# Talking-heads attention and a mixture of experts on one core: first transfers over two queues, six score buffers, due times a step sooner, loads by their use

## The chip, the cores and the metric

The kernel runs on 1 core of one Trainium2 chip. The metric is the device time of one execution in microseconds, the median of several runs; lower is better.

## The reference, cut to what matters

```python
# q, k, v: (4, 12, 448, 64); w_pre, w_post: (12, 12)
scores = (q @ k.transpose(0, 1, 3, 2)) / sqrt(64)
scores = einsum('bhij,hg->bgij', scores, w_pre)      # pre-mix: heads mixed ahead of the softmax
scores = scores - max(scores, -1)
attn = exp(scores); attn = attn / (sum(attn, -1) + 1e-9)
attn = einsum('bhij,hg->bgij', attn, w_post)         # post-mix: heads mixed behind it
x = (attn @ v)                                       # as 1792 tokens of 768
# then: x goes to one of 8 experts, the arg max of cosine similarities over tau
out[mask] = gate[mask] * (relu(x[mask] @ w1[e]) @ w2[e])
```

All of it is float32. The change touches the attention alone.

## The kernel before

**Tiles and pairs.** The 448 query rows of each of the 4 batches are cut into 4 tiles of 120, 120, 120 and 90 rows: 16 tiles (`NTL`). The 12 heads are taken as 6 pairs a tile: 96 pairs. `emit_qk` (L228) computes the scores of one pair, four matmuls into two PSUM banks: one `ps_q` tile (one buffer), or, in the opening for odd pairs, two `ps_p` tiles (two buffers of one bank). Its `evict` copies them into a score buffer `s` (`s_p`, 4 buffers, L139), on ACT, or for odd pairs of the opening on DVE. Its `place` (L247) sends that buffer with two DMAs on SP's queue, one for each head, into the tile's group buffer (`group(t)`, one of three), in which partitions hold (query row within ten, head), so that the heads can be mixed by a matmul. A group buffer is written again for a later tile once the tile before it in that buffer is read.

**Steps.** Each tile is then read in steps of 20 query rows (6, 6, 6 and 5 steps, 92 in all, `steps`; `first[t]` is tile t's first: 0, 6, 12, 18, 23, 29, ...). For step s: `emit_pre` (L261) mixes the heads into `ps_p`, `emit_max` takes row maxima on DVE (L274), `emit_exp` exponentials on ACT with row sums (L283), `emit_r` the reciprocals on DVE and with them the post weights `wr` on GpSimd (L294), `emit_post` (L299) mixes again and transposes on TensorE, DVE copies the result to `a` (L322), `emit_av` multiplies by v a tile later.

**Opening.** Lines 729 to 759 are in the order in which each engine gets its instructions: q of tile 0 and the six k of batch 0 on SP; 8 filler matmuls (`NWARM`); then `N0` = 9 pairs, each evicted and placed while the next is computed, with q of tile 1 loaded on SP after the placing of pair 2 (`i == 3`); q of tile 2, the ninth pair's placing, four loads of v; 20 filler matmuls (`NWAIT`); then pre-mix, maximum and exponentials of step 0, the same of step 1, and the reciprocals of step 0.

**The loop over steps** (L768): all engines run in order, and the order is written out by hand. In step s: up to one pair ahead of, and one behind, the rest; `emit_pre(s + 2)`; the copy of step s - 1; that pair's eviction and placing; `emit_post(s)`; `emit_max` and `emit_exp` of s + 2; work of the tile before; at its end the loads listed in `bg` for this step. How many pairs are due by step s is the largest of `N0 + s + 1`, of `due(s)` (L760), which wants the last pair of tile t in step first[t] - 4, and of 96 + 3 (s - `OPEN`) // 2, which has all 96 done in step `OPEN` = 79, when the buffers of q, k and s are given up for expert weights. Loads are listed by L697 to L705: q of tile t (from 3 on) in step 6 t - N0 - 6, k of pair a in step 6 t + a - N0 - 6, the four parts of v in steps first[t + 1] - 6 to first[t + 1] - 3.

**Queues.** SP issues every load and every score transfer in the order of the program; a DMA whose target or source isn't free yet holds up those behind it.

Of the kernel before, what the change touches and what calls it, by code (L numbers as in the profile page):

```python
# [7 lines left out]
F32 = mybir.dt.float32  # L8
# [18 lines left out]
NTL = 4 * B  # L27
# [4 lines left out]
LEAD = 2  # L32
N0 = 9
NWAIT = 20
XW = 128 + E
# [9 lines left out]
def talking_heads_moe(  # L45
# [79 lines left out]
    with tc.manual_schedule():  # L125
# [12 lines left out]
        q_p = bx.enter_context(tc.tile_pool(name="q", bufs=3, side="right"))  # L138
        s_p = bx.enter_context(tc.tile_pool(name="s", bufs=4, side="right"))  # L139
        ve_p = bx.enter_context(tc.tile_pool(name="ve", bufs=1, side="right"))  # L140
# [23 lines left out]
        def embed():  # L164
# [41 lines left out]
            V.tensor_scalar(out=ioE_v, in0=ioE_v, scalar1=1.0, scalar2=None, op0=ALU.add)  # L206

        q_sb, k_sb, v_sb = {}, {}, {}

# [18 lines left out]
        def emit_qk(i, eng, pre=False):  # L228
# [10 lines left out]
            def evict():  # L239
                sb = s_p.tile([128, 2, S], F32, tag="s", name="s")  # L240
                for o, i in [(sb, pq[:, :, :S])] if pq is not None else [(sb[:, r], p[r][:, :S]) for r in range(2)]:
                    if eng is A:
                        A.activation(out=o, in_=i, func=ACTF.Copy)  # L243
                    else:
                        V.tensor_copy(out=o, in_=i)

                def place():  # L247
                    for r in range(2):
                        h = 4 + 2 * a + r
                        Y.dma_start(out=group(t)[h:h + 109:12, :n // 10].rearrange("p c s -> p (c s)"), in_=sb[:n, r])  # L250
                return place
# [8 lines left out]

        def emit_pre(s):  # L261
            t, m, nx = steps[s]
            p = [ps_p.tile([128, 512], F32, tag="p", name="p_p") for _ in range(2)]
            g = group(t)
# [432 lines left out]
        for t in range(NTL):  # L697
            b, ti = divmod(t, 4)
            if t:
                bg_at(max(6 * t - N0 - 6, 0), lambda t=t: load_q(t)) if t > 2 else None  # L700
            if ti == 0 and b:
                for a in range(NPAIR):
                    bg_at(max(6 * t + a - N0 - 6, 0), lambda b=b, a=a: load_k(b, a))
                for jt in range(4):
                    bg_at(first[t + 1] - 6 + jt, lambda b=b, jt=jt: load_v(b, jt))  # L705
# [34 lines left out]
        for g in gb[1:]:  # L740
            G_.memset(g[:4], 0.0)
        pend = []
        for i in range(N0):
            pend.append(emit_qk(i, V if i % 2 else A, i % 2 == 1))
            if i:
                pend.pop(0)()()
            if i == 3:
                load_q(1)
        load_q(2)
        pend.pop()()()  # L750
        for jt in range(4):
# [3 lines left out]
        for s in range(LEAD):  # L755
            emit_pre(s)
            emit_max(s)
            emit_exp(s)
        run(emit_r(0))
        def due(s):  # L760
            n = [min(NPAIR * t + NPAIR, NPAIR * t + s + 10 - first[t]) for t in range(NTL) if s > first[t] - 10]
            return n + [NTL * NPAIR + 3 * (s - OPEN) // 2]

        qk_n = N0
        evict = None
        ea = None
        gv = None
        for s in range(ns):  # L768
            cr = emit_r(s + 1) if s + 1 < ns else iter(())
            evs = []  # L770
            want = min(NTL * NPAIR, max(N0 + s + 1, *due(s)))
            assert want - qk_n < 3
            if qk_n < want:
                evs.append(emit_qk(qk_n, A))
                qk_n += 1
# [5 lines left out]
            if evs:  # L781
                evs.pop()()()
            evict = emit_post(s)
# [9 lines left out]
            if evs:  # L793
                evs.pop()()()
            for f in pes.pop(s, ()):
# [357 lines left out]
```

## Time and profile before

| | us |
|---|---|
| median of 3 runs | 762.78 |
| lowest and highest of them | 761.76, 764.29 |
| the profiled execution | 760.22 |
| its span, first to last instruction | 758.4 |

The profile is of one execution. Its page gives busy times, the span in slices, DMA queues and the costliest groups of instructions; the trace can be asked for waits, for a timeline and for windows. PE is TensorE's matmuls, PEld its weight loads, DVE VectorE, ACT ScalarE, POOL GpSimd; a "q" behind an engine's name is its queue, which issues DMAs. Matmuls of float32 are recorded twice, as two passes. TensorE's two clock levels are 1.2 and 2.4 GHz; "granted" is the share of the higher one.

### The profile page before, as it was taken

What the parts mean: (1) busy time and instruction counts of PE and PEld (TensorE: products, weight loads), DVE (VectorE), ACT (ScalarE), POOL (GpSimd) and SP (SyncE); (2) the same over time, 40 slices, a digit from 0 to 9 for tenths busy, and PEclk for the clock granted to TensorE, in tenths of its full rate; (3) what the DMA queues carried; (4) which work ended last, traced back from release to release, by engine and by line L of the source; (5) the groups of instructions that cost most, each with busy time, mean ns of one, the idle gap of its engine ahead of it and who ended that gap; (6) DMA issues with size and microseconds to landing.
All of it is one profiled execution on the core that took longest, in us unless ns stands there. A gap on an engine that the chain in (4) does not pass through costs nothing. (4 is left out here: it accounts for less than half of the span.)

```text
span 758.4 us, 26020 instructions
## 1 busy us (share of the span) xinstructions
PE 698.4 (92%) x11146; PEld 569.0 (75%) x11146; DVE 462.5 (61%) x1083; ACT 392.9 (52%) x767; POOL 118.1 (16%) x179
## 2 busy tenths in 40 slices
PE   5889999899999999969888978999999999999984
PEld 2557677566766767745566757999999999999973
DVE  3287666565765656634797464676866556565661
ACT  2366667566766766745444433453434436353550
POOL 9011100001000110100201024202020221201010
PEclk9899999999999999998989999999999999999997
DMA  6754555646556465662513172776758576756760
GB/s 201 235 159 150 168 160 170 201 134 173 177 176 179 131 202 171 189 191 85 190 56 85 56 254 74 224 242 206 233 184 260 185 253 187 239 193 194 228 208 15
DMA packets 55414, 133.09 MB, mean 175 GB/s; under 512 B 6519, under 2 KB 31239, under 8 KB 55296
## 3 DMA queue, kind: packets, MB, share of 16 engines
q1 hardware_dynamic: 51744, 118.94, 51.0%
q0 software_dynamic: 3520, 12.44, 5.0%
q8 instruction: 89, 1.46, 0.8%
q14 instruction: 29, 0.24, 0.1%
q10 hardware_dynamic: 32, 0.01, 0.0%
HBM read 81.64 MB, written 12.20 MB: 124 GB/s over the span
## 5 line engine op out<-in xcount | busy, mean ns | idle before, releaser
L274 DVE TENSOR_REDUCE mn<-p_p 128x1 f32<-128x448 f32 (+1 forms) x184 | 106.6, 618 | 120.1 <-PE p_p L266 119.7
L550 ACT ACTIVATE wh<-raw_w 128x768 fp32r<-128x768 f32 (+2 forms) x132 | 115.1, 904 | 52.5 <-DMA raw_w<-w 46.5
L283 ACT ACTIVATE e<-p_p,mn 128x448 f32<-128x448 f32 (+1 forms) x184 | 114.9, 629 | 49.2 <-DVE mn L274 44.9
L243 ACT ACTIVATE s<-p_q 128x896 f32<-128x896 f32 x92 | 84.4, 917 | 106.6 <-PE p_q L236 86.3
L551 DVE TENSOR_TENSOR wl<-raw_w,wh 128x768 fp32r<-128x768 f32 (+2 forms) x132 | 130.9, 1027 | 12.1 <-ACT wh L550 11.5
L309 PEld LDWEIGHTS p_m<-wr,e 64*64 64x64 f32 x4320 | 97.3, 137 | 51.6 <-issue 47.4
L236 PE MATMUL p_q<-k,q 64*64 64x448 f32 x768 | 97.8, 577 | 17.5 <-DMA q<-qT 14.7
L309 PE MATMUL p_m<-wr,e 64*64 64x60 f32 x4320 | 99.8, 224 | 8.3 <-DVE a L322 6.5
L266 PE MATMUL p_p<-g,wpre_sb 64*64 64x448 f32 (+1 forms) x720 | 93.0, 555 | 7.4 <-DMA v<-vP 3.5
L322 DVE COPY a<-p_m 128x420 f32<-128x420 f32 (+1 forms) x184 | 98.1, 574 | 0.8 <-PE p_m L314 0.7
L944 PE MATMUL p_h<-xh,wh 128*128 128x256 f32 x336 | 96.6, 288 | 0.0
L335 PE MATMUL p_av<-a,v 128*64 128x120 f32 (+1 forms) x1536 | 96.1, 271 | 0.0
L944 PE MATMUL p_h<-xh,wl 128*128 128x256 f32 x336 | 94.8, 282 | 0.0
L944 PE MATMUL p_h<-xl,wh 128*128 128x256 f32 x336 | 94.5, 281 | 0.0
L294 POOL TENSOR_TENSOR wr<-wpost_sb,r 128x120 f32<-128x120 f32 (+1 forms) x92 | 35.3, 383 | 348.2 <-DVE r L293 314.8
L335 PEld LDWEIGHTS p_av<-a,v 128*64 128x64 f32 x1536 | 76.7, 140 | 10.9 <-issue 5.4
L962 PE MATMUL p_o<-wh,hh 128*128 128x384 f32 x224 | 75.6, 338 | 0.0
L962 PE MATMUL p_o<-wl,hh 128*128 128x384 f32 x224 | 74.9, 334 | 0.0
L962 PE MATMUL p_o<-wh,hl 128*128 128x384 f32 x224 | 74.9, 334 | 0.0
L946 ACT ACTIVATE hh<-p_h 128x512 fp32r<-128x512 f32 x28 | 16.8, 598 | 100.8 <-PE p_h L944 79.9
L266 PEld LDWEIGHTS p_p<-g,wpre_sb 64*64 64x64 f32 (+1 forms) x720 | 30.0, 135 | 48.6 <-issue 28.4
L944 PEld LDWEIGHTS p_h<-xl,wh 128*128 128x128 f32 x336 | 63.6, 189 | 0.0
(205 smaller groups left out, 989.5 us busy)
## 6 DMA issues: line engine op xcount, KB each, us to landing
g<-s SPq DMA_DIRECT2D x144, 210.0 KB
raw_w<-w SPq DMA_DIRECT2D x54, 512.0 KB
raw_w<-w SPq DMA_DIRECT2D x72, 384.0 KB
g<-s SPq DMA_DIRECT2D x48, 157.5 KB
q<-qT SPq DMA_DIRECT2D x16, 384.0 KB
v<-vP SPq DMA_DIRECT2D x16, 384.0 KB
k<-kT SPq DMA_DIRECT2D x24, 224.0 KB
x_tok<-xs SPq DMA_DIRECT2D x12, 360.0 KB
```

The source lines that it names most:

```text
L236: T.matmul(p[r][64 * w:64 * w + 64, :S], q_sb[t][64 * r:64 * r + 64, a, w, :], k_sb[t // 4, a][64 * r:64 * r + 64], start=True, stop=True)
L243: A.activation(out=o, in_=i, func=ACTF.Copy)
L266: T.matmul(p[w][64 * x:64 * x + 64, :S], wpre_sb[64 * w:64 * w + 64 - 4 * w], g[64 * w:64 * w + 64 - 4 * w, m + x if nx == 2 else m], star ...
L274: V.tensor_reduce(out=mn[q, c:c + 1], in_=p[u][q, :S], op=ALU.max, axis=AX.X, negate=True)
L283: A.activation(out=e[q, c], in_=p[u][q, :S], func=ACTF.Exp, bias=mn[q, c:c + 1], accum_out=sums[q, c:c + 1])
L309: T.matmul(pm[x][q[c], u * 210 + jt * 60:u * 210 + jt * 60 + 60], e[q[x], u, jt * 128 + 64 * c:jt * 128 + 64 * c + 64], wr[q[x], u], start ...
L322: V.tensor_copy(out=a[:, :, m + x] if n == 2 else a[:, :, m, x], in_=src if n == 2 else src[:, :, 0])
L335: T.matmul(p[64 * r:64 * r + 64], v_sb[t // 4][:, jt, (2 * a + r) * D:(2 * a + r + 1) * D], a_sb[t % 2][:, c:c + n], start=jt == 0, stop=j ...
L550: A.activation(out=h[:, c], in_=r[:, c], func=ACTF.Copy)
L551: lo = lambda: eng.tensor_tensor(out=l[:, c], in0=r[:, c], in1=h[:, c].bitcast(F32), op=ALU.subtract)
L944: T.matmul(p[:, f], lt[:, c], rt_[:, k], start=(k == 0 and i == 0), stop=(k == KD - 1 and i == 2))
L962: T.matmul(p[:, :384], lt[:, k, c], rt_[:, m], start=(k == 0 and i == 0), stop=(k == KF - 1 and i == 2))
```

## The change

- `N0` is 10 and `NWAIT` 8.
- The score buffers `s` are 6.
- `place` takes a second queue for the second of its two DMAs: ACT's for the six pairs of tile 0, SP's as before for all others.
- q of tile 1 is loaded ahead of the opening's loop.
- In the opening both pre-mixes come first, the second into a `ps_q` tile, then maximum and exponentials of step 0, the reciprocals of step 0, maximum and exponentials of step 1.
- In the due times, 11 stands for 10: the last pair of a tile is due in step first[t] - 5. Step 0 has no pair ahead of its pre-mix.
- Score transfers go on a list (`held`) and are issued in order once the step has come (`free`) in which the last pre-mix of the tile before in the same group buffer is issued.
- `qk_at` holds the step in which each pair is computed, and q and k are loaded six steps before.

```diff
--- before.py
+++ after.py
@@ -30,8 +30,8 @@
 MAXO = 12
 NPAIR = H // 2
 LEAD = 2
-N0 = 9
-NWAIT = 20
+N0 = 10
+NWAIT = 8
 XW = 128 + E
 OPEN = 79
 NW = 4
@@ -136,7 +136,7 @@
         sm = ax.enter_context(tc.tile_pool(name="sm", bufs=4))
         k_p = bx.enter_context(tc.tile_pool(name="k", bufs=9, side="right"))
         q_p = bx.enter_context(tc.tile_pool(name="q", bufs=3, side="right"))
-        s_p = bx.enter_context(tc.tile_pool(name="s", bufs=4, side="right"))
+        s_p = bx.enter_context(tc.tile_pool(name="s", bufs=6, side="right"))
         ve_p = bx.enter_context(tc.tile_pool(name="ve", bufs=1, side="right"))
 
         gb = [p.tile([128, c, S], F32, name=f"g{i}") for i, (p, c) in enumerate(((ve_p, 12), (big, 12), (big, 9)))]
@@ -205,6 +205,19 @@
             yield
             V.tensor_scalar(out=ioE_v, in0=ioE_v, scalar1=1.0, scalar2=None, op0=ALU.add)
 
+        def due(s):
+            n = [min(NPAIR * t + NPAIR, NPAIR * t + s + 11 - first[t]) for t in range(NTL) if s > first[t] - 11]
+            return min(NTL * NPAIR, max(N0 + s + 1, NTL * NPAIR + 3 * (s - OPEN) // 2, *n))
+
+        def free(i):
+            t = i // NPAIR
+            back = 4 if t % 4 == 3 else 2 if t % 4 == 2 else 3
+            return first[t - back + 1] - 1 - LEAD if t >= back else 0
+
+        qk_at = [0] * N0
+        for s in range(OPEN + 1):
+            qk_at += [s] * (due(s) - len(qk_at))
+
         q_sb, k_sb, v_sb = {}, {}, {}
 
         def load_q(t):
@@ -244,10 +257,10 @@
                     else:
                         V.tensor_copy(out=o, in_=i)
 
-                def place():
+                def place(second=Y):
                     for r in range(2):
                         h = 4 + 2 * a + r
-                        Y.dma_start(out=group(t)[h:h + 109:12, :n // 10].rearrange("p c s -> p (c s)"), in_=sb[:n, r])
+                        (second if r else Y).dma_start(out=group(t)[h:h + 109:12, :n // 10].rearrange("p c s -> p (c s)"), in_=sb[:n, r])
                 return place
             return evict
 
@@ -258,9 +271,13 @@
             return [(slice(0, 128), u, u) for u in range(2)] if steps[s][2] == 2 else [
                 (slice(64 * w, 64 * w + 64), w, 0) for w in range(2)]
 
-        def emit_pre(s):
+        def emit_pre(s, pair=False):
             t, m, nx = steps[s]
-            p = [ps_p.tile([128, 512], F32, tag="p", name="p_p") for _ in range(2)]
+            if pair:
+                pq = ps_q.tile([128, 2, 512], F32, tag="q", name="p_q")
+                p = [pq[:, r] for r in range(2)]
+            else:
+                p = [ps_p.tile([128, 512], F32, tag="p", name="p_p") for _ in range(2)]
             g = group(t)
             for x, w in [(x, w) for w in range(2) for x in range(2)] if nx == 2 else [(0, 0), (1, 1)]:
                 T.matmul(p[w][64 * x:64 * x + 64, :S], wpre_sb[64 * w:64 * w + 64 - 4 * w],
@@ -697,10 +714,10 @@
         for t in range(NTL):
             b, ti = divmod(t, 4)
             if t:
-                bg_at(max(6 * t - N0 - 6, 0), lambda t=t: load_q(t)) if t > 2 else None
+                bg_at(max(qk_at[6 * t] - 6, 0), lambda t=t: load_q(t)) if t > 2 else None
             if ti == 0 and b:
                 for a in range(NPAIR):
-                    bg_at(max(6 * t + a - N0 - 6, 0), lambda b=b, a=a: load_k(b, a))
+                    bg_at(max(qk_at[6 * t + a] - 6, 0), lambda b=b, a=a: load_k(b, a))
                 for jt in range(4):
                     bg_at(first[t + 1] - 6 + jt, lambda b=b, jt=jt: load_v(b, jt))
         acts, dves, pes, avs = {}, {}, {}, {}
@@ -739,38 +756,37 @@
         next(ge)
         for g in gb[1:]:
             G_.memset(g[:4], 0.0)
+        load_q(1)
         pend = []
         for i in range(N0):
             pend.append(emit_qk(i, V if i % 2 else A, i % 2 == 1))
             if i:
-                pend.pop(0)()()
-            if i == 3:
-                load_q(1)
+                pend.pop(0)()(A if i <= NPAIR else Y)
+        pend.pop()()()
         load_q(2)
-        pend.pop()()()
         for jt in range(4):
             load_v(0, jt)
         for _ in range(NWAIT):
             T.matmul(p_w[:, :128], ones_sb, ones_sb, start=True, stop=True)
         for s in range(LEAD):
-            emit_pre(s)
+            emit_pre(s, s == 1)
+        for s in range(LEAD):
             emit_max(s)
             emit_exp(s)
-        run(emit_r(0))
-        def due(s):
-            n = [min(NPAIR * t + NPAIR, NPAIR * t + s + 10 - first[t]) for t in range(NTL) if s > first[t] - 10]
-            return n + [NTL * NPAIR + 3 * (s - OPEN) // 2]
-
+            if s == 0:
+                run(emit_r(0))
         qk_n = N0
+        held = []
+        placed = N0
         evict = None
         ea = None
         gv = None
         for s in range(ns):
             cr = emit_r(s + 1) if s + 1 < ns else iter(())
             evs = []
-            want = min(NTL * NPAIR, max(N0 + s + 1, *due(s)))
+            want = due(s)
             assert want - qk_n < 3
-            if qk_n < want:
+            if qk_n < want and s:
                 evs.append(emit_qk(qk_n, A))
                 qk_n += 1
             if s + LEAD < ns:
@@ -779,7 +795,10 @@
                 evict()
             next(cr, None)
             if evs:
-                evs.pop()()()
+                held.append(evs.pop()())
+            while held and free(placed) <= s:
+                held.pop(0)()
+                placed += 1
             evict = emit_post(s)
             next(cr, None)
             if qk_n < want:
@@ -791,7 +810,10 @@
                 emit_max(s + LEAD)
                 emit_exp(s + LEAD)
             if evs:
-                evs.pop()()()
+                held.append(evs.pop()())
+                while held and free(placed) <= s:
+                    held.pop(0)()
+                    placed += 1
             for f in pes.pop(s, ()):
                 f()
             for f in dves.pop(s, ()):
```

## Rows read from the trace of the kernel before

**Rows 1.** The page: busy us of each engine, share of the span, instructions
```profile
PE 698.4 (92%) x11146; PEld 569.0 (75%) x11146; DVE 462.5 (61%) x1083; ACT 392.9 (52%) x767; POOL 118.1 (16%) x179
```
**Rows 2.** Windows: stretch, length, busy us (instructions) of each engine, granted clock, DMA share, GB/s
```profile
60.00:136.00 76.00, 75.51 (x1932) 53.74 (x1926) 50.91 (x134) 52.39 (x120) 7.39 (x20) 1.00 0.57 168
...
380.00:400.00 20.00, 17.59 (x370) 13.40 (x370) 17.86 (x62) 9.75 (x28) 1.55 (x4) 0.83 0.17 49
```
**Rows 3.** TensorE's waits, 0 to 420 us: waiter, releaser, us in total, times, longest
```profile
PE p_q L236 <- DMA q<-qT: 14.7, 2, 9.0
...
PE p_p L266 <- DMA v<-vP: 3.5, 2, 2.0
```
**Rows 4.** DMA issues: what, queue, operation, count, KB each
```profile
g<-s SPq DMA_DIRECT2D x144, 210.0 KB
...
q<-qT SPq DMA_DIRECT2D x16, 384.0 KB
...
k<-kT SPq DMA_DIRECT2D x24, 224.0 KB
```
**Rows 5.** Timeline of the opening: start, us, engine, instruction, [idle time before <-releaser]
```profile
4.86 1.95 PE L236 MATMUL p_q<-k,q 64*64 64x448 f32 x16
...
12.56 1.57 SPq L212 DMA_DIRECT2D q<-qT  x1
12.89 0.92 ACT L243 ACTIVATE s<-p_q 128x896 f32<-128x896 f32 x1 [3.83 <-DMA g<-s]
14.24 11.84 SPq L250 DMA_DIRECT2D g<-s  x10
16.52 1.16 DVE L245 COPY s<-p_q 128x448 f32<-128x448 f32 x2 [6.51 <-DMA g<-s]
...
19.99 4.76 PE L236 MATMUL p_q<-k,q 64*64 64x448 f32 x24 [8.96 <-DMA q<-qT]
...
24.68 5.26 PE L754 MATMUL p_w<-ones_sb 128*128 128x128 f32 x40
...
29.87 0.98 PE L266 MATMUL p_p<-g,wpre_sb 64*64 64x448 f32 x8
```
**Rows 6.** Windows of the opening, columns as in rows 2
```profile
0.00:10.00 10.00, 8.55 (x58) 5.25 (x60) 4.57 (x9) 3.12 (x3) 8.86 (x14) 1.00 0.63 207
...
3.00:7.00 4.00, 3.78 (x25) 2.19 (x24) 2.09 (x2) 0.88 (x1) 4.00 (x2) 1.00 1.01 358
8.00:18.00 10.00, 2.94 (x28) 0.91 (x22) 2.31 (x4) 1.83 (x2) 10.00 (x8) 0.88 0.62 180
...
22.00:24.00 2.00, 2.00 (x16) 0.44 (x8) 0.72 (x2) 0.78 (x1) 0.00 (x0) 0.50 0.68 240
...
15.60:25.80 10.20, 5.81 (x29) 2.45 (x30) 2.31 (x4) 1.83 (x2) 3.04 (x1) 0.50 0.69 205
```
**Rows 7.** Timeline of ACT's queue, DMA issues
```profile
404.83 2.07 ACTq L450 DMA_DIRECT2D g_tok<-gt__7091  x3
```
**Rows 8.** Timeline of the first steps
```profile
34.94 0.39 POOL L294 TENSOR_TENSOR wr<-wpost_sb,r 128x120 f32<-128x120 f32 x1 [16.30 <-DVE r L293]
```
**Rows 9.** Timeline at late pre-mixes; last, a group of lines, 60 to 330 us
```profile
139.33 0.98 PE L266 MATMUL p_p<-g,wpre_sb 64*64 64x448 f32 x8 [1.95 <-DMA v<-vP]
...
233.05 0.98 PE L266 MATMUL p_p<-g,wpre_sb 64*64 64x448 f32 x8 [0.40 <-DMA g<-s]
...
323.79 0.98 PE L266 MATMUL p_p<-g,wpre_sb 64*64 64x448 f32 x8 [1.53 <-DMA v<-vP]
...
L274 DVE TENSOR_REDUCE mn<-p_p 128x1 f32<-128x448 f32 (+1 forms) x135 | 78.3, 619 | 92.7 <-PE p_p L266 92.6
```
**Rows 10.** Timeline and windows around pair 90
```profile
337.32 0.50 SPq L212 DMA_DIRECT2D q<-qT  x1
342.03 1.77 PE L236 MATMUL p_q<-k,q 64*64 64x448 f32 x8 [5.71 <-DMA q<-qT]
...
342.00:346.70 4.70, 4.67 (x80) 2.81 (x80) 1.38 (x4) 2.02 (x5) 0.00 (x0) 0.50 0.06 19
```

## The prediction

> **What bounds the kernel now.** I read the page's busy shares first: TensorE is busy for 92% of the span [rows 1], so a change that moves no arithmetic can only win back stretches in which TensorE stands still or runs at the lower clock. The windows by stretch tell where those are: from 60 to 136 us TensorE is busy 75.51 of 76 us, in the opening and late in the attention it is not [rows 2, 6]. The list of TensorE's waits up to 420 us, longest first, names them: 14.7 us for the loads of q in two places, and 3.5 us in front of a pre-mix (L266), for DMAs that the list names v [rows 3]. The timeline puts a place on each. In the opening TensorE waits 8.96 us for q of tile 1 at 19.99, then runs 20 filler matmuls (40 records, 5.26 us) and reaches the first pre-mix at 29.87 [rows 5]. Three first pre-mixes of a tile start late, at 139.33, 233.05 and 323.79, with 1.95, 0.40 and 1.53 us of idle time [rows 9]. At 342.03 the score matmul of pair 90 has waited 5.71 us for q of tile 15 [rows 10]. Elsewhere TensorE is the bound itself, so time that is won ahead of such a stretch is kept; nothing after it starts by a clock of its own.
>
> **A. The opening.** What must land before the first pre-mix can run is q and k of the first batch, 384 + 6 x 224 KB, q of tile 1 where it is queued ahead, and the 12 transfers of the six score pairs of tile 0, 210 KB each [rows 4].
> The kernel before spends this way: SP issues the transfers of three pairs, then q of tile 1 at 12.56, then ten more up to 26.08 [rows 5]. ACT's fifth eviction and DVE's third wait 3.83 and 6.51 us for a score buffer whose transfer has not landed [rows 5]: four buffers throttle the issue. The pairs 6 to 8 wait for q, and behind them stand the fillers. So before, no single thing is the bound; it is a relay of three.
> After the change q of tile 1 stands at about 4 us in SP's queue, straight behind k; the six pairs of tile 0 have a buffer each, so no eviction of tile 0 waits for a landing; one transfer of each such pair goes through ACT's queue.
> How soon can all of it have landed? From 0 to 10 us 207 GB/s were moved, 2.07 MB [rows 6], of which q and k are 1.77 MB, so some 0.3 MB are others' (GpSimd's loads and the first scores). Left at 10 us are about 12 x 0.215 + 0.39 - 0.25 = 2.7 MB, and some 0.15 MB of GpSimd's small loads. At 205 GB/s, as from 15.6 to 25.8 us [rows 6], that is 14 us, landing at 24; at 240, the best stretch [rows 6], 12 us, landing at 22. I take 23.
> Is TensorE there by then? Even pairs share one PSUM buffer, so each takes its matmuls (0.98, as eight matmuls of that width take [rows 9]) and its eviction (0.92 on ACT [rows 5]) in turn, 2.0 us with the hand-over; for the first six pairs ACT issues two transfers between two of its evictions. An issue on ACT is seen here only late in the run, 0.69 us each for far smaller transfers [rows 7]; on SP the score issues are 1.2 us apart (11.84 / 10) [rows 5]. I take 0.8: 5 x 2.0 + 6 x 0.8 = 14.8 us from 4.86, so the tenth pair is scored at about 19.7, and 8 fillers (16 records of 0.13 us) end at 21.8. ACT's issues are thus hidden behind the landing at 23; with 1.2 us each they cost 2.4 us more and the fillers end at 24.2. Below nothing they can't go, since they only add to ACT's queue, in which evictions and exponentials stand behind them.
> First pre-mix at 23.0 instead of 29.87: **-6.9 us**. Bounds: -3.2 (only the twelve fillers less, 24 records of 0.13 us; then it starts at 26.7) and -8.1 (landing hidden, TensorE's own 21.8).
> Behind it, the second pre-mix no longer waits for the exponentials of the first, but its maximum now stands on DVE behind the reciprocal of step 0, which waits for the same exponentials, so it starts hardly sooner. What does come sooner is the post weight: GpSimd made it at 34.94, 5.1 us after the first pre-mix [rows 8], now about 3.5 after. The 1.5 us shorten the first steps only in part, since their chain runs over DVE; 0.5 us. Against it stands the clock: granted 0.50 from 15.6 to 25.8 [rows 6] after TensorE's long wait, and back at 1.00 before the first pre-mix. With the first pre-mix at 23 some of the first steps may run at half rate, 0 to 1.5 us. The two I set at zero together.
>
> A page of the Trainium skill speaks against the second queue ("DMA: Bandwidth & Descriptors", section "Issuing engines are not separate DMA queues"): transfers issued from SP and from ACT run on the same 16 DMA engines, so a second queue saves issue time alone. Its section on why a DMA increments its semaphore by 16 adds that a transfer whose outer dimensions are 120 and 10 is spread over ten of them, the lowest-numbered. The trace agrees: while loads of 128 rows move, the DMA share is 1.01 at 358 GB/s; while scores move it stays at 0.62 to 0.68 with 180 to 240 GB/s, near ten sixteenths [rows 6]. By the Trainium skill's page a rate of 358 with two queues is out (landing at 18, TensorE's 21.8 deciding); by my rows alone it stays a bound.
>
> **B. Buffers, holding and order in the steady part.** A transfer of scores is now issued only in a step in which the last reader of its place has been issued. Before, it stood at the head of SP's queue and everything behind it waited; by the schedule this touches only the first pair of the third tile of each batch (12, 36, 60, 84), held one step. Six buffers cover that. I cost it at nothing; what hides it is that those pairs are read six or more steps later. Were the buffers to run out, ACT's eviction would wait with the exponentials behind it.
>
> **C. The last pair of a tile a step sooner.** With N0 = 10 and the 11 in the due times, pair 35 is scored in step 24, not 25, pair 59 in 48, not 49, pair 83 in 71, not 72, and read by the first pre-mix of tiles 5, 9 and 13, in steps 27, 50 and 73. A step has 4.0 us in the mean (135 maxima, two a step, in 270 us [rows 9]), so the transfer starts some 4 us sooner and the idle times of 1.95, 0.40 and 1.53 us [rows 9] go: **-3.9 us**. The four loads of v, a batch's worth, stay where they are in SP's queue, so part of the wait could stay: bound -1.9. The step with two pairs only moves one step up (14, 37, 60 become 13, 36, 59); nothing either way. What is late next there is TensorE's own work.
>
> **D. q and k by their use.** q of tile 15 was issued at the end of step 75 (6 x 15 - 9 - 6), but pair 90 is scored in step 76, since the due times before step 79 run ahead: 96 + (3 x (76 - 79)) // 2 = 91 pairs. SP issued it at 337.32 behind four score transfers; TensorE had it at 342.03 [rows 10]. Now it is issued in step 70, six steps ahead, some 24 us, against the 4.7 us it took. The 5.71 us go, and with them what follows from them: after the idle stretch the granted clock is 0.50 from 342.0 to 346.7 [rows 10], and eight matmuls take 1.77 us, not 0.98 [rows 10]. At the full clock, TensorE being the bound, the 4.7 us would be 2.35. 5.71 + 2.35 = 8.1: **-8.1 us**; bound -5.7, if the clock falls anyway. k is loaded two to three steps sooner into buffers free by then (k of batch 1, pair 3 waits for pair 18, scored in step 8; its load is in step 10): nothing. After step 79 the work is unchanged; DVE is busy 17.86 of 20 us from 380 to 400 [rows 2], and TensorE's idle times there stay.
>
> **The sum**: -6.9 - 3.9 - 8.1 = -18.9 us. Against the profiled execution's 760.22 that is 741.3; the median shown is 762.78, 2.56 above it, so I forecast **743.9**.
>
> **Rivals.**
> *R1: the scores of the opening land no sooner.* Their number, their size and their ten or so engines are the same; q of tile 1 now goes ahead of them. The sixth of the ten issues from 14.24 stands at about 21.3 (0.6 x 11.84), and with the 4.7 us of q of tile 15 it lands at 26. For it: the flat DMA share. Against it: 3.83 and 6.51 us in which two evictions waited, so the queue was not kept full. Then A is -3.2: 747.6. By the page of the Trainium skill that is named above, the queue itself gives nothing, and R1 is what is left if buffers and order don't fill the gaps.
> *R2: a new wait takes the place of one in C or D*: q is there, but the places of pairs 84 to 89, or the v loads, hold TensorE. C gone and D at 5.7: 750.2; D kept to half: 752.
> *R3: not what it says*: SP works in order, and a held or blocked transfer ahead of q of tile 15 keeps its issue late. Then -10.8: 752.
> *R4: slower.* Score transfers stay out longer because up to six pairs are under way beside k and q, all on the same DMA engines; the first pre-mix of each of 15 tiles waits as that of 139.33 does. At 1.95 us it costs 29 us against 18.9 won: 773. It decides once a tile's last transfer lands more than three steps, some 12 us, after its issue. Against it: a DMA share of 0.57 from 60 to 136 us [rows 2], and before only three of these 15 pre-mixes waited, by two steps' margin [rows 9].
>
> **How the numbers follow.** Forecast with its own range (738 to 746.5) 0.60, R1 0.22, R2 and R3 together 0.10, no measurable change 0.03, R4 0.05. The clock's drops after 360 us may fall otherwise in a changed program, 2 us either way. The range 738 to 751 leaves about 2 in 10 out: the far ends of the forecast, part of R2 and R3, and R4. A measurement of this kernel tells 0.3%, 2.3 us, from no change; faster by more: 0.60 + 0.22 + 0.10 = 0.92, within 0.03, slower 0.05.
>
> **What would show it.** A: the first pre-mix at 22 to 24 us, no wait for q in the opening, ACT's issues there at about 0.8 us, the DMA share of 10 to 22 us still at 0.6 to 0.7. (Above 0.8 the rule of the Trainium skill's page would not hold here.) C: no idle time over 0.4 us ahead of the first pre-mixes of tiles 5, 9 and 13. D: no wait for q near 325 us and a granted clock of 1.00 there. I am wrong if TensorE waits for scores in front of other tiles, or if the first pre-mix stands at 26 or later.

## The result and the profile after

| | before | after |
|---|---|---|
| median, us | 763.09 | 743.27 |
| lowest and highest | 761.76, 764.29 | 740.09, 745.60 |
| the profiled execution | 760.22 | 745.50 |
| its span | 758.4 | 743.6 |

The change makes the kernel faster: the ratio of the times is 0.9738, with an interval of 0.9688 to 0.9787. The medians differ by 19.8 us, the two profiled executions by 14.7; the forecast was 743.9 (738 to 751), from a sum of -18.9.

TensorE's row of the page after (busy us, share of the span, instructions), which answers to [rows 1], and its waits from 0 to 420 us (waiter, releaser, total, times, longest), which answer to [rows 3]:

```profile
PE 693.0 (93%) x11122; PEld 565.6 (76%) x11122; DVE 464.0 (62%) x1085; ACT 392.1 (53%) x766; POOL 118.0 (16%) x179
...
PE p_q L249 <- ACT s L256: 7.2, 8, 2.1
PE p_m L326 <- DVE a L339: 5.7, 6, 2.1
PE p_m L326 <- issue: 3.9, 4, 2.5
...
PE p_p L283 <- DMA g<-s: 1.5, 1, 1.5
PE p_m L331 <- issue: 1.4, 1, 1.4
PE p_q L249 <- DMA k<-kT: 1.1, 1, 1.1
```

The 14.7 us for q are gone, and so are the 3.5 us in front of a pre-mix; what is left of DMA waits is 1.5 us for the very first scores and 1.1 for a k of the opening. Longer is "issue", 3.9 and 1.4 us (the kernel before has 1.6, 0.8 and 0.6): TensorE stands still while nothing that this list shows holds it.

The opening after, as a timeline (start, us, engine, instruction, [idle time before <-releaser]), answers to [rows 5] and [rows 8]:

```profile
4.02 0.43 SPq L225 DMA_DIRECT2D q<-qT  x1
7.58 18.00 SPq L263 DMA_DIRECT2D g<-s  x14
7.58 2.58 ACTq L263 DMA_DIRECT2D g<-s  x2
11.15 2.21 ACTq L263 DMA_DIRECT2D g<-s  x2
14.36 1.91 ACTq L263 DMA_DIRECT2D g<-s  x2
19.01 2.05 PE L770 MATMUL p_w<-ones_sb 128*128 128x128 f32 x16
22.56 0.98 PE L283 MATMUL p_p<-g,wpre_sb 64*64 64x448 f32 x8 [1.50 <-DMA g<-s]
23.57 1.16 DVE L291 TENSOR_REDUCE mn<-p_p 128x1 f32<-128x448 f32 x2 [3.30 <-PE p_p L283]
25.89 1.13 DVE L291 TENSOR_REDUCE mn<-p_q 128x1 f32<-128x448 f32 x2
26.06 0.39 POOL L311 TENSOR_TENSOR wr<-wpost_sb,r 128x120 f32<-128x120 f32 x1 [7.40 <-DVE r L310]
```

q of tile 1 is issued at 4.02, no wait for it is left, all ten pairs are scored when the fillers start at 19.01, and TensorE waits 1.50 us for the scores: the landing is last, as forecast, at 22.56 against 23.0. (e1 shows how far this differs between executions.) The six issues on ACT's queue take (2.58 + 2.21 + 1.91) / 6 = 1.1 us each, between the 0.8 that I took and the 1.2 of the bound. The post weight comes 3.5 us after the first pre-mix, as said.

The windows after (length, busy us (instructions) of PE, PEld, DVE, ACT, POOL, granted clock, DMA share, GB/s) answer to [rows 6] and, the last, to [rows 10]:

```profile
12.00:18.00 6.00, 3.30 (x36) 1.01 (x32) 2.31 (x4) 1.83 (x2) 6.00 (x2) 1.00 0.67 240
18.00:24.00 6.00, 4.50 (x44) 2.62 (x36) 1.58 (x3) 0.92 (x1) 0.66 (x1) 1.00 0.67 238
...
324.00:330.00 6.00, 6.00 (x158) 3.87 (x154) 2.84 (x7) 4.17 (x9) 0.39 (x1) 1.00 0.45 137
```

The DMA share is 0.67, within the 0.6 to 0.7 that were named, and the rate 240 GB/s, the upper of the two that I took. Where TensorE waited for q of tile 15 it is now busy without a gap at the full clock.

Where the time went can be read from one mark a step, the start of the first maximum of a step (L274 before, L291 after; 92 of them in each trace). The stretches add up to the whole difference of the spans:

| from the maximum of step | before | after | difference | part |
|---|---|---|---|---|
| start to 0 | 30.89 | 23.57 | -7.32 | A |
| 0 to 11 | 36.34 | 36.80 | +0.46 | A |
| 11 to 12 | 4.42 | 6.13 | +1.71 | a stall |
| 12 to 28 | 62.18 | 62.00 | -0.18 | |
| 28 to 29 (tile 5) | 6.50 | 8.54 | +2.04 | C, and a stall |
| 29 to 51 | 87.91 | 85.36 | -2.55 | |
| 51 to 52 (tile 9) | 5.81 | 4.55 | -1.26 | C |
| 52 to 74 | 84.79 | 85.43 | +0.64 | |
| 74 to 75 (tile 13) | 5.96 | 4.20 | -1.76 | C |
| 75 to 78 | 20.51 | 13.08 | -7.43 | D |
| 78 to 91 | 60.74 | 60.35 | -0.39 | |
| 91 to the end | 352.35 | 353.59 | +1.24 | |

In these two executions A gave 6.9 (forecast 6.9), D 7.4 (8.1), C only 1.0 net (3.9), and the rest cost 0.5: 14.8 us. The two stalls are these, on the timeline, with the windows of the second:

```profile
62.64 0.31 PE L331 MATMUL p_m<-wr,e 64*64 64x30 f32 x5 [1.43 <-issue]
131.70 0.28 PE L326 MATMUL p_m<-wr,e 64*64 64x60 f32 x5 [2.54 <-issue]
...
129.00:132.70 3.70, 1.16 (x33) 1.02 (x26) 1.20 (x4) 1.34 (x4) 0.00 (x0) 1.00 0.88 269
132.70:136.10 3.40, 3.40 (x31) 1.89 (x33) 0.80 (x4) 0.00 (x0) 0.39 (x1) 0.50 0.88 232
```

TensorE does 1.16 us of work in 3.7 us, and the 3.4 us behind that run at the lower of its two clocks, 1.2 GHz. The wait of [rows 9] at tile 5 is gone, and this stands one step ahead of its place. The kernel before had such a stall too, 1.57 us in the stretch from 29 to 51.

### The profile page after: what moved, and what is told of

It reads as the page before. It is cut to its first block, busy times and chain, and to the rows that moved or that the text cites. A ratio compares the mean times of both kernels' runs of the same rounds, so it can differ in the third digit from the quotient of the medians.

```text
span 743.6 us, 25975 instructions
## 1 busy us (share of the span) xinstructions
PE 693.0 (93%) x11122; PEld 565.6 (76%) x11122; DVE 464.0 (62%) x1085; ACT 392.1 (53%) x766; POOL 118.0 (16%) x179
## 5 line engine op out<-in xcount | busy, mean ns | idle before, releaser
L291 DVE TENSOR_REDUCE mn<-p_p 128x1 f32<-128x448 f32 (+1 forms) x182 | 105.3, 618 | 100.9 <-PE p_p L283 100.6
L249 PE MATMUL p_q<-k,q 64*64 64x448 f32 x768 | 95.0, 567 | 9.3 <-ACT s L256 7.2
L283 PE MATMUL p_p<-g,wpre_sb 64*64 64x448 f32 (+1 forms) x712 | 90.8, 549 | 2.2 <-DMA g<-s 1.5
L966 PEld LDWEIGHTS p_h<-xh,wl 128*128 128x128 f32 x336 | 63.2, 188 | 0.0
```

The source lines that it names most:

```text
L249: T.matmul(p[r][64 * w:64 * w + 64, :S], q_sb[t][64 * r:64 * r + 64, a, w, :], k_sb[t // 4, a][64 * r:64 * r + 64], start=True, stop=True)
L283: T.matmul(p[w][64 * x:64 * x + 64, :S], wpre_sb[64 * w:64 * w + 64 - 4 * w], g[64 * w:64 * w + 64 - 4 * w, m + x if nx == 2 else m], star ...
L291: V.tensor_reduce(out=mn[q, c:c + 1], in_=p[u][q, :S], op=ALU.max, axis=AX.X, negate=True)
L966: T.matmul(p[:, f], lt[:, c], rt_[:, k], start=(k == 0 and i == 0), stop=(k == KD - 1 and i == 2))
```

## The experiments

All but e4 start from the kernel after. Where stretches are compared they are taken between the marks of the table. Several of these kernels have only four timed executions, which lie up to 15 us apart; the intervals of e2, e6, e7, e8, e9 and e11 overlap that of the kernel after (0.9688 to 0.9787), so their times show no difference from it, and their traces show waits rather than worths.

**e1: the kernel after, unchanged, again.**

> The changed kernel once more, nothing edited. Its four times so far lie in two pairs, 740.1 and 741.1, 745.5 and 745.6; the profiled one (745.5) has two stretches in which TensorE stands still with nothing named as the cause, 1.43 us before 62.64 and 2.54 us before 131.70, and the clock at half after the second. Theory: these stalls fall in other places in each execution, and 4 to 5 us between executions come from them; then this trace has the same first pre-mix (22.6 +- 0.3 us) and none of these two stalls, or others. Rival: they belong to the program's order; then they stand at the same places, 62.6 and 131.7 +- 1 us.

Measured: 743.75 us (six executions, 741.15 to 754.98), ratio 0.974 (0.9711 to 0.9769); the profiled execution took 750.3. Its timeline, and its windows:

```profile
28.49 1.77 PE L283 MATMUL p_p<-g,wpre_sb 64*64 64x448 f32 x8 [5.21 <-DMA g<-s]
71.13 0.31 PE L331 MATMUL p_m<-wr,e 64*64 64x30 f32 x5 [2.34 <-issue]
139.91 0.28 PE L326 MATMUL p_m<-wr,e 64*64 64x60 f32 x5 [2.27 <-issue]
...
12.00:18.00 6.00, 2.14 (x24) 0.56 (x20) 2.31 (x4) 1.83 (x2) 6.00 (x2) 1.00 0.65 207
18.00:24.00 6.00, 5.28 (x32) 3.38 (x32) 1.16 (x2) 0.92 (x1) 0.64 (x1) 0.72 0.66 185
```

Three things follow. The stalls stand at the same two instructions of the program (steps 11 to 12 and 28 to 29), so they belong to the program and not to an execution. The opening differs by 5.9 us between two executions of the same kernel: at nearly the same DMA share, 0.65 to 0.67, 207 and 185 GB/s were moved instead of 240 and 238, and the first pre-mix came at 28.49 instead of 22.56. The maximum of step 11 stands at 67.9 us here, at 60.4 in the other execution and at 67.2 in the kernel before, so in this one nothing of A is left. And the three stretches of C give 3.2 us here, not 1.0: behind the stall of 139.91 the granted clock stays at 1.00.

**e2: one queue.**

```diff
-                pend.pop(0)()(A if i <= NPAIR else Y)
+                pend.pop(0)()()
```

> All transfers of tile 0 from SP's queue, as before the change; the rest of the change stays. Theory (the ten or so engines that scores use set the pace, not the issue): first pre-mix at 22.6 +- 0.5 us, DMA share of 8 to 22 us still 0.62 to 0.68, time as the changed kernel's within 1 us; evictions on ACT a little sooner, as it issues nothing. Rival (two queues bring the transfers in sooner): first pre-mix at 24.5 to 26, time 2 to 3.5 us longer.

Measured: 746.17 us (four executions, 739.17 to 751.72), ratio 0.976 (0.9686 to 0.9834); profiled 744.49, 1.0 below the kernel after's own. Timeline and windows:

```profile
23.26 1.77 PE L283 MATMUL p_p<-g,wpre_sb 64*64 64x448 f32 x8 [4.02 <-DMA g<-s]
...
12.00:18.00 6.00, 5.53 (x44) 2.09 (x40) 2.31 (x4) 2.21 (x3) 6.00 (x2) 1.00 0.67 232
18.00:24.00 6.00, 1.98 (x16) 1.38 (x18) 1.16 (x2) 0.00 (x0) 0.64 (x1) 0.87 0.64 221
```

From SP alone the scores land 0.7 us later than in the kernel after, at nearly the same DMA share (0.67 and 0.64); TensorE and ACT are done sooner, as ACT issues nothing, and TensorE waits 4.02 us, behind which its clock is down and the maximum of step 11 comes 1.9 us later. Both are far inside the 5.9 us of e1, so no gain of the second queue is shown, and the rival's 24.5 to 26 us didn't come. This agrees with the Trainium skill's page "DMA: Bandwidth & Descriptors", section "Issuing engines are not separate DMA queues", by which a second issuing engine saves issue time alone.

**e3: q and k loaded as before, all else of the change kept.**

```diff
-  bg_at(max(qk_at[6 * t] - 6, 0), lambda t=t: load_q(t))
+  bg_at(max(6 * t - 15, 0), lambda t=t: load_q(t))
-  bg_at(max(qk_at[6 * t + a] - 6, 0), lambda b=b, a=a: load_k(b, a))
+  bg_at(max(6 * t + a - 15, 0), lambda b=b, a=a: load_k(b, a))
```

> q and k loaded by the fixed steps of the kernel before (q of tile t in step 6 t - 15); the rest of the change stays. Theory: TensorE waits 5 to 6 us for q of tile 15 at pair 90 again, with half the clock behind it, 8 us in all: 751.3. Rival (the wait went because score transfers no longer stand ahead of q in SP's queue): at most 2 us, 743 to 745.

Measured: 756.69 us (seven executions, 751.91 to 767.55), ratio 0.9916 (0.9877 to 0.9955), so D taken back costs 12.9 us where the theory had 8. The timeline:

```profile
264.87 0.98 PE L249 MATMUL p_q<-k,q 64*64 64x448 f32 x8 [1.01 <-DMA k<-kT]
271.38 1.77 PE L249 MATMUL p_q<-k,q 64*64 64x448 f32 x8 [2.90 <-DMA k<-kT]
285.27 0.98 PE L249 MATMUL p_q<-k,q 64*64 64x448 f32 x8 [0.83 <-DMA k<-kT]
314.98 1.43 PE L249 MATMUL p_q<-k,q 64*64 64x448 f32 x8 [2.17 <-DMA q<-qT]
341.23 1.77 PE L249 MATMUL p_q<-k,q 64*64 64x448 f32 x8 [5.13 <-DMA q<-qT]
```

The wait of [rows 10] is back, and there are four more: since C takes the pairs a step sooner, their loads are now late in other places too. From step 52 to 74 this kernel takes 95.1 us against 85.4, from 74 to 78 22.8 against 17.3. D is the ground on which C stands, which the forecast had not seen.

This kernel shows one thing more. Its TensorE stream is that of the kernel after, only the loads differ, and from step 11 to 12 it takes 4.43 us, without the stall. In the kernel after the k of batch 1 are issued at 55.68, 58.70 and 62.61, around the stall; here first at 64.82.

**e4: D alone, in the kernel before.**

```diff
+        qk_at = [0] * N0
+        for s in range(OPEN + 1):
+            qk_at += [s] * (min(NTL * NPAIR, max(N0 + s + 1, *due(s))) - len(qk_at))
-  bg_at(max(6 * t - N0 - 6, 0), lambda t=t: load_q(t))
+  bg_at(max(qk_at[6 * t] - 6, 0), lambda t=t: load_q(t))
-  bg_at(max(6 * t + a - N0 - 6, 0), lambda b=b, a=a: load_k(b, a))
+  bg_at(max(qk_at[6 * t + a] - 6, 0), lambda b=b, a=a: load_k(b, a))
```

> The kernel before with one part of the change alone: q and k loaded six steps before the step that uses them. Theory: the wait at pair 90 and the half clock behind it go, 8.1 us, and nothing after takes the time back: 755.0. Rival (a later stage waits instead): 759 to 763.

Measured: 755.57 us (six executions, 753.31 to 758.03), ratio 0.9936 (0.9898 to 0.9973), 7.0 below the 762.61 of the kernel before, timed beside it; by the ratio it is 4.9 (2.1 to 7.8). No wait for q is left behind the opening, but the three pre-mixes of [rows 9] wait longer:

```profile
139.42 1.31 PE L274 MATMUL p_p<-g,wpre_sb 64*64 64x448 f32 x8 [2.63 <-DMA v<-vP]
232.67 0.98 PE L274 MATMUL p_p<-g,wpre_sb 64*64 64x448 f32 x8 [1.24 <-DMA v<-vP]
327.96 1.77 PE L274 MATMUL p_p<-g,wpre_sb 64*64 64x448 f32 x8 [4.47 <-DMA g<-s]
```

They wait 8.3 us together where it was 3.88: the likely reason is that loads moved ahead now stand in front of score transfers in SP's queue (in front of tile 5, q is issued ahead of the transfers at 137.79; behind them in the kernel before), which was not tested by itself. So D alone wins a little less than its own sum said and hands some of it to waits ahead of tiles 5, 9 and 13.

**e5 and e12: the due times of before, all else kept.** The two are the same kernel; the times of e5 lie 13 us apart, and e12 repeats it.

```diff
-  n = [min(..., NPAIR * t + s + 11 - first[t]) for t in range(NTL) if s > first[t] - 11]
-  return min(NTL * NPAIR, max(N0 + s + 1, NTL * NPAIR + 3 * (s - OPEN) // 2, *n))
+  n = [min(..., NPAIR * t + s + 10 - first[t]) for t in range(NTL) if s > first[t] - 10]
+  return min(NTL * NPAIR, max(N0 + s, NTL * NPAIR + 3 * (s - OPEN) // 2, *n))
```

> The changed kernel with the due times of the kernel before (each pair in the step in which it was scored there; the opening still scores ten). Theory: what took the three waits away is the step that the last pair of a tile comes sooner; without it TensorE waits again in front of the first pre-mixes of tiles 5, 9 and 13, at least 1.9, 0.4 and 1.5 us, and more where the loads that now come sooner are in the way (2.6, 1.2 and 4.5 us with these loads alone), 4 to 8 us in all: 747 to 752. Rival: holding the transfers back and six buffers took them away; then no such wait and 743 to 745.

> Again the changed kernel with the due times of the kernel before (last pair of a tile due in step first[t] - 4), all else of the change kept; the first execution of it that was profiled had a slow opening. Theory: with the loads by their use and the old due times the pairs of tiles 9 and 13 come just behind their first pre-mix's need, as in the kernel before with the loads alone (1.24 and 4.48 us in front of the first pre-mixes of tiles 9 and 13, 2.63 of tile 5). So here the first pre-mixes of tiles 9 and 13 wait 2 to 5 us each for g, where the changed kernel waits for none, and from the maximum of step 7 to that of step 85 it takes 322 to 328 us, where the four profiled executions of the changed kernel and of its kin with whole loads by use took 316 to 318; the time is 750 to 754 us. Rival: the waits of the first execution (2.64 and 3.77) followed from its slow opening; then, with an opening that lands at 23 to 25 us, no such wait is over 1 us, the stretch takes 316 to 318 us, and the time is within 2 us of 743.5.

Measured: e5 757.55 us (752.41 to 765.68), ratio 0.9898 (0.9806 to 0.999); e12 754.76 (749.6 to 757.61), ratio 0.9891 (0.9831 to 0.9951): against the 0.9738 of the kernel after, C taken back costs some 12 us by either ratio. The timeline of e12:

```profile
137.54 0.26 PE L331 MATMUL p_m<-wr,e 64*64 64x30 f32 x4 [2.13 <-issue]
234.22 0.98 PE L283 MATMUL p_p<-g,wpre_sb 64*64 64x448 f32 x8 [1.71 <-DMA v<-vP]
241.30 0.27 PE L326 MATMUL p_m<-wr,e 64*64 64x60 f32 x2 [2.43 <-issue]
329.92 1.77 PE L283 MATMUL p_p<-g,wpre_sb 64*64 64x448 f32 x8 [3.75 <-DMA g<-s]
```

The waits in front of tiles 9 and 13 are back; that of tile 9 is 1.71, a little under the 2 that the theory asked for. From step 7 to 85 it takes 326.0 us, against 316.4 in the kernel after and 316.7 in e1: the theory's 322 to 328 holds, the rival's 316 to 318 does not. Of these 9.6 us, 7.9 stand in steps 51 to 52 (+1.58) and 74 to 77 (+6.31), where C acts. Its time is 0.8 us above the theory's 750 to 754. Since six buffers and the holding are kept here, they are not what takes these two waits away. In front of tile 5 no DMA wait came back, in e5 or in e12; there TensorE's own stall, 2.13 us, stands as in the kernel after, so that C removed the wait of tile 5 is not shown.

**e6: four score buffers.**

```diff
-        s_p = bx.enter_context(tc.tile_pool(name="s", bufs=6, side="right"))
+        s_p = bx.enter_context(tc.tile_pool(name="s", bufs=4, side="right"))
```

> The changed kernel with four score buffers. Theory: tile 0's own evictions no longer wait for a landing even with four, since its pairs are evicted 3 us apart and a transfer lands in 4 to 5; the pairs behind it wait, and the first pre-mix comes 1 to 2 us later (23.5 to 24.5 where the scores land as in the changed kernel): 744 to 746. Rival: the buffers carry the gain of the opening; evictions 4 and 5 wait 3 us or more each and the first pre-mix stands at 26 or later: 747 to 749.

Measured: 747.42 us (740.49 to 749.44), ratio 0.9773 (0.9689 to 0.9857). Evictions wait for landings again, as in [rows 5]:

```profile
14.54 1.16 DVE L258 COPY s<-p_q 128x448 f32<-128x448 f32 x2 [4.04 <-DMA g<-s]
19.01 1.16 DVE L258 COPY s<-p_q 128x448 f32<-128x448 f32 x2 [3.31 <-DMA g<-s]
20.68 0.92 ACT L256 ACTIVATE s<-p_q 128x896 f32<-128x896 f32 x1 [2.96 <-DMA g<-s]
```

The first pre-mix starts at 24.71, at 231 to 233 GB/s; that is 2.2 us behind the kernel after and 1.5 behind e2, whose rate was like its own, and TensorE does not wait in front of it: with the evictions held up, its own work is last. So of the theory the time of the first pre-mix nearly came, but not its reason, since tile 0's evictions do wait; of the rival the waits came, but not the 26 us. From step 7 to 85 it takes 318.4 us against 316.4: behind the opening the two buffers are worth little.

**e7 and e8: q of tile 1 issued later**, behind three pairs' transfers as in the kernel before (e7), or behind two pairs' (e8).

```diff
-        load_q(1)
...
+            if i == 3:
+                load_q(1)
```

That is e7; e8 has its two lines in the same loop with `i == 2`.

> The changed kernel with q of tile 1 loaded behind the placing of pair 2, as before. Theory: TensorE waits for it again, some 3 us, in the opening, scores the tenth pair at about 24 and reaches the first pre-mix at 26 instead of 22.6: 746.5. Rival: the landing of tile 0's scores sets the first pre-mix, and they land 1 us sooner without q ahead of them: 21.6, 742.5.

> The changed kernel with q of tile 1 loaded behind the placing of pair 1. Theory: what the ten or so engines have to move ahead of tile 0's last scores shrinks by q's share, 1 us; q still lands by 16, when the seventh pair wants it: first pre-mix 1 us sooner than in the changed kernel at the same rate (2.9 MB at 240 GB/s: 21.6). Rival: the load waits in SP's queue behind four score transfers, lands after 17, and TensorE waits for it: first pre-mix at 23 or later.

Measured: e7 748.64 us (737.93 to 749.82), ratio 0.9732 (0.9619 to 0.9846); e8 750.09 (742.03 to 750.29), ratio 0.9824 (0.9742 to 0.9907). The row of e7 and then of e8:

```profile
20.57 5.47 PE L249 MATMUL p_q<-k,q 64*64 64x448 f32 x32 [8.40 <-DMA q<-qT]
...
18.50 5.47 PE L249 MATMUL p_q<-k,q 64*64 64x448 f32 x32 [6.29 <-DMA q<-qT]
```

Each kernel waits for q again, 8.40 and 6.29 us, more than the 3 us that the theory of e7 had, and the four pairs behind it run at the lower clock in part. The first maximum comes at 28.96 and 28.34, 5.4 and 4.8 us behind the kernel after, but ahead of the 30.28 of e1. Even two pairs ahead of q make TensorE wait. How much of the later maximum is the rate of landing (201 to 221 GB/s in e8 from 12 to 24 us) can't be split off; the wait itself is shown, its worth is not.

**e9: 20 fillers.**

```diff
-NWAIT = 8
+NWAIT = 20
```

> The changed kernel with 20 fillers instead of 8. Theory: where the scores land by 22.6, the fillers end at 24.3 (24 records of 0.13 us more, from 21.1) and cost 1.7 us: 745; where they land later, the fillers cost nothing. Rival (fewer fillers leave TensorE at half the clock in the first steps): with 20 the clock stays at 1.00 from 20 to 40 us and the time is 1 us shorter.

Measured: 749.31 us (746.78 to 750.56), ratio 0.9811 (0.9754 to 0.9868). Timeline and windows:

```profile
24.38 0.98 PE L283 MATMUL p_p<-g,wpre_sb 64*64 64x448 f32 x8 [0.26 <-DMA g<-s]
...
34.00:38.00 4.00, 4.00 (x84) 2.39 (x80) 3.52 (x16) 2.13 (x6) 0.39 (x1) 0.57 0.71 214
```

The first pre-mix comes 1.8 us later than after, and TensorE hardly waits for it: with 20 fillers they are last, with 8 the landing is. The fillers buy no clock: it falls to 0.57 from 34 to 38 us anyway, as the kernel after's did not in that stretch. The twelve more fillers moved the stalls: none over 0.25 us is left in step 11, one of 1.0 us stands at 131.12, and about 2 us each at 223.52, 255.76 and 299.32, where the kernel after has none.

**e10: the first two pre-mixes in one buffer, as before.**

```diff
-            emit_pre(s, s == 1)
-        for s in range(LEAD):
+            emit_pre(s)
```

> The changed kernel with the second pre-mix of the opening in the PSUM tiles of the first, so that it waits for the exponentials of step 0. Theory: the maximum of step 1 starts about 3.4 us after the first pre-mix in both, since it stands behind the reciprocal of step 0; from the first maximum to the fourth (30.9 to 40.7 before, 23.6 to 34.5 in the changed kernel) there is at most 0.7 us between the two. Rival: separate banks are worth the exponential's 1.4 us, and this one is that much longer.

Measured: 750.94 us (737.49 to 752.16). Its times lie 15 us apart. From its first maximum to its fourth it takes 13.52 us, at a granted clock of 0.75; e1 takes 10.88 at 0.81, e11 11.34 at 0.80, and the kernel after 10.88 at 1.00. So this execution is 2.2 us or more longer, not the theory's 0.7 at most and more than the rival's 1.4. It is one execution, and the stretch of the kernel before, with one buffer, was 9.81 at 1.00, so what the second bank is worth stays open.

**e11: the loads of v spread.**

```diff
-  bg_at(first[t + 1] - 6 + jt, lambda b=b, jt=jt: load_v(b, jt))
+  bg_at(first[t + 1] - 13 + 2 * jt, lambda b=b, jt=jt: load_v(b, jt))
```

> The changed kernel with the four loads of v of each later batch in every second step from first[t + 1] - 13 on, not in four steps in a row from first[t + 1] - 6. Theory: TensorE's stalls without a named cause (2.54 us before 131.70 and the half clock behind it) are its code loading waiting behind the burst of v and scores; spread, the stall of step 27 goes or falls below 1 us: 739.5 where the scores land as in the changed kernel. Rival: they hang on the place in TensorE's stream alone; the stall of step 27 stays at 2.3 to 2.6 us and the time is 743.

Measured: 747.09 us (739.62 to 749.64), ratio 0.9787 (0.9707 to 0.9867). A stall of 2.01 us still stands at 140.82, in the same step (28 to 29), below the rival's 2.3 to 2.6 but not below the theory's 1. So the v loads queued just ahead of it are not its cause, or not alone.

What the stalls are can be read by counting. Beside the loads a queue named "instruction" moves packets of about 16 KB. Up to each of the two stalls of the kernel after, the windows from 0 give the number of TensorE's matmul records, and the DMA view of the same stretch the number of these packets:

```profile
0.00:62.63 62.63, 48.98 (x977) 1.00 0.69 221
q8 instruction: 7, 0.11, 0.8%
...
0.00:131.69 131.69, 115.20 (x2622) 1.00 0.62 192
q8 instruction: 20, 0.33, 1.0%
```

Between the stalls lie 13 packets and 1645 matmuls, 126.5 to a packet. The 14 traces have 67 idle times of TensorE of over 0.25 us from 45 to 345 us for which nothing is named ("issue"). Each stands behind 90 + 126.6 n matmuls, to within four, where n is the number of packets that have come by then, and ends 2.2 to 3.2 us behind the n-th packet. e9 tells the count from the place in the program: its stream has 24 matmul records more in the opening (12 fillers, recorded twice), and its stall of step 28 still stands behind 2622, which is 24 records earlier in the program:

```profile
0.00:131.11 131.11, 119.47 (x2622) 0.99 0.61 189
```

So in these stalls TensorE waits for its own code, which comes a packet at a time. A late packet is needed for a long one: the 29 stalls of 1 us or more have packets that came 6.3 to 9.6 us behind the one before, where 5 us is usual. It is not enough, since the packets of 172.6 and 181.5 us in the kernel after lie 8.9 us apart and no stall is there.

What makes a packet late is shown in part. The seventh (step 11) is waited for in all eight profiled kernels that have the loads and the TensorE stream of the kernel after behind the opening, 0.35 us (e2) to 2.64 (e11), and in none of e3, e5 and e12, which issue the first k of batch 1 a step or two later; so k being under way ahead of it is the likely cause. The twentieth (step 28) is waited for in all twelve kernels with the new opening, 1.0 to 2.67 us, with either timing of k, of v and of the pairs; what holds it up stays open.

## Why the prediction was right, and where it was not

**The time** is right, 743.9 against 743.27, and in part by luck. The sum was -18.9 and the two spans differ by 14.8. The medians lie 5.1 us further apart than the profiled executions because the one before is 2.9 below its median and the one after 2.2 above.

**A** came out as summed in the profiled execution: 22.56 against 23.0, landing last, TensorE's own work hidden, no wait for q, and the post weight and the first steps' clock cancel to +0.46 by step 11. That the size fits is luck too. Seven profiled kernels issue the same work up to the first pre-mix; it stood at 22.56 (the kernel after), 24.49 (e3), 25.28 (e10), 26.94 (e11), 27.61 (e12), 28.23 (e5) and 28.49 us (e1), with 181 to 240 GB/s. In four of the seven it is behind 26, which the forecast had named as the sign of being wrong. The maximum of step 11 stands at 67.2 us in e11 and 67.9 in e1, against 67.2 in the kernel before and 66.4 in e4, so in these two A is worth nothing. The step that failed is the rate: the 23 was taken between landings at 22 and 24, from 240 and 205 GB/s, two stretches of one trace.

Of A's mechanism the waits are shown: with four buffers evictions wait for landings (e6), with q later TensorE waits for q (e7, e8), with 20 fillers TensorE's own work is last (e9). What each is worth is not: the first pre-mixes of these four, 24.38 to 27.95 us, lie inside the spread of the unchanged opening. The second queue, which the forecast let stand among the causes, shows no gain (e2). No run takes the whole opening back, or `N0` alone. How often the timed executions have the one landing or the other was not measured; their spread (741 to 750 us for five of the six in e1) is of that size.

**B** was right for the steady part: the kernel after waits for no scores behind its opening, and four buffers instead of six change steps 7 to 85 by 2 us. The holding alone was not tested.

**C** is the term that was mis-sized, in both directions. I priced it by the waits of the kernel before, 1.95 + 0.40 + 1.53. The last two went (-1.26 and -1.76 with what follows them), but at tile 5 TensorE's own stall of 2.54 us and 3.4 us at the lower clock stood in the place of the DMA wait, and the net is -1.0 (-3.2 in e1). The stall is no work of C: e5 and e12 have it with the old due times. In the presence of D, however, C is worth some 12 us (e5, e12), since D's sooner loads lengthen the waits that C removes (e4: 3.88 became 8.3). The forecast summed three terms as if they were independent.

**D** was right: no wait for q, clock 1.00, -7.4 against -8.1, and alone in the kernel before -7.0 by the medians or -4.9 by the ratio (e4). The step that failed stands at its end: "k is loaded two to three steps sooner into buffers free by then ...: nothing". With those loads around step 11 the kernel after waits 1.43 us for its code there (2.34 in e1), and e3, with k later and the same TensorE stream, does not.

**The rest**: 18.9 were summed and 14.8 seen between the two spans. The missing 4.1 are C's 2.9, D's 0.7, the stall of step 11 to 12 with 1.7 and 1.2 us behind step 91, less 2.5 in the other stretches (most of it from step 29 to 51, where the kernel before had its own stall of 1.57).

**The rivals.** R1 did not hold in the profiled execution of the kernel after, but in four of the seven profiled openings the scores landed later than its 26 us. R2 came in part: a new wait took the place of one in C, but TensorE's for its own code, not one for places or v. R3 and R4 fell: q of tile 15 came in time, and behind 40 us no pre-mix waits.

## What to carry to other kernels

Loads timed by their use and transfers issued a step sooner are one edit, not two: they share a queue, and with either taken back the time rose by 12 to 13 us (e3, e5, e12), where they had been priced at 8.1 and 3.9. So price them together, by who then stands last in the queue. Where a landing was the bound and the DMA share stayed flat, a second issuing engine showed no gain. Where TensorE stands still and nothing is named, count its matmuls up to the stall and the instruction packets: if both go up together, it waits for its code. And before calling a gain or a loss in one profile a fact, profile the same kernel again: the opening alone moved by 5.9 us.

## What the runs showed of the hardware that I had not expected

The rate at which the scores land differs between executions that issue the same work, 181 to 240 GB/s from 12 to 24 us, while the DMA share stays at 0.63 to 0.67. TensorE loses up to 2.7 us at a time waiting for its own code, which comes in packets of 16 KB, one for every 126.6 matmul records and as many weight loads; all 67 nameless stalls in 14 traces stand at such a border and end 2.2 to 3.2 us behind the packet. Where they fall goes by the count of TensorE's instructions (e9), and one went when loads moved (e3). Behind a stall the granted clock can be 0.50 for 3.4 us (the kernel after, 132.7 to 136.1) or stay at 1.00 (e1, 139.9 to 143.5). An issue of a 210 KB transfer on ACT's queue took 1.1 us, during which ACT evicts nothing.
